# Layer one by products of halves, layer two with four hidden sums a tile pair, and a written-out step order, in a sigmoid attention and feed-forward kernel

## Chip, cores and metric

One core of a Trainium2 chip runs the whole program. The metric is the time on the device in microseconds, the median of several executions; beside it stands one execution that the hardware profiler recorded.

## What is computed

Sigmoid attention over 8 batches, 12 heads, 448 positions and 64 dimensions a head; its output, laid out as 3584 tokens of 768 values, goes through two dense layers with a gate between them. Inputs and output are float32 in HBM.

```python
scores = scale * q @ k.T - log(S)              # S = 448
attn   = sigmoid(scores) @ v                   # per batch and head
x      = attn.transpose(0, 2, 1, 3).reshape(3584, 768)
h      = x @ w_in                              # 768 -> 2048
g      = h * sigmoid(beta * h)
out    = g @ w_out                             # 2048 -> 768
```

## The kernel before

All matmuls run in fp16 with float32 sums. Heads are taken four at a time, a quad `g`; three quads make a batch `b`, 24 quads in all. For a quad, `transpose` (VectorE) turns the loaded q and k; `visit(g, jt)` makes the scores of key block `jt`: matmuls on 32 rows of the array, four side by side, into two score tiles (two PSUM buffers of two banks each), and `weigh` lets ScalarE apply the sigmoid into an `attnT` tile. `attend(g)` multiplies these with v, column tiles of 64, and VectorE casts the result into `xT`, which has six chunks of 128 channels by 448 tokens for a batch.

Layer one is `dense1(b, dc)`: for one of 16 blocks of 128 hidden columns, six matmuls of 448 columns (one a channel chunk) into a PSUM bank, a sigmoid on ScalarE and a multiplication on VectorE into `gt`. `gt` holds 896 tokens, seven tiles of 128, so batches alternate between its halves. For batch 0 the tokens are taken in two halves of 224.

Layer two takes token tiles in pairs. Tiles 0 and 1 are multiplied directly (`dense2`). Every later pair goes by Strassen's seven products of halves (`strassen`): the hidden dimension (16 blocks) and the 768 output columns are halved, each product is eight matmuls of 384 columns; weight sums T1, T3, T4, T6, T7 are formed once by `weight_sum`, five hidden sums a pair by `hidden_sum` on VectorE. Products are put together in `osb` on VectorE (one copy on ScalarE), then stored by DMAs that SP issues.

PSUM has four banks beside the score tiles; `bank` gives out the least recently used one that is not held, and `release` gives a held one back.

The order is fixed by the program. After the first batch's attention, a planner goes through the visits in order and puts filler work between them: a stream of `dense1`, `dense2` and `strassen` units with costs `M1_US`, `M1H_US`, `M2_US`, spread by a budget. Between the last visit of a quad and its `attend`, `dense` is cut into 64-column tiles (`tiled["cols"]`), as attention is. Each engine works through its own queue in program order. q, k, v and the weights are loaded by DMAs that POOL issues; before the change POOL does nothing else but a few memsets.

Of the kernel before, what the change touches and what calls it, by code (L numbers as in the profile page):

```python
# [8 lines left out]
FP32 = mybir.dt.float32  # L9
# [4 lines left out]
def kernel(  # L14
# [41 lines left out]
    qTp = ctx.enter_context(tc.tile_pool(name="qTp", bufs=4))  # L56
    kTp = ctx.enter_context(tc.tile_pool(name="kTp", bufs=4))
    attnp = ctx.enter_context(tc.tile_pool(name="attnp", bufs=12))
    xTp = ctx.enter_context(tc.tile_pool(name="xTp", bufs=3))
    sump = ctx.enter_context(tc.tile_pool(name="sump", bufs=3))  # L60
    sigp = ctx.enter_context(tc.tile_pool(name="sigp", bufs=3))
# [31 lines left out]
    beta_in = const.tile([BLK, P], FP32, name="beta_in")  # L93
# [128 lines left out]
    def weigh(sco, n: int):  # L222
        at = attnp.tile([P, 2, S], FP16, tag="attnT", name="attnT")
        nc.scalar.activation(  # L224
            out=at[:, :, 0:n],
            in_=sco[:, :, 0:n],
            func=AF.Sigmoid,
            bias=NEG_LOG_S,
            scale=MSCALE,
        )  # L230
        return at
# [18 lines left out]
    def half_visit(g: int, c0: int, second: int):  # L250
# [13 lines left out]
        ats = {id(sco): weigh(sco, n) for sco, n in zip(scos, widths)}  # L264
# [53 lines left out]

    def dense2(t: int, half: int, part: int):
        lo, hi = half * HALF, (half + 1) * HALF  # L320
        if part == 0:
            m2s[t, half] = bank("m2_ps", hi - lo, (t, half))
        m2 = m2s[t, half]
        for dc in range(part * NDC // N2, (part + 1) * NDC // N2):
            dense(
                m2,
                gt[:, dc, cols(t)],
                w_out16[:, dc, lo:hi],
                start=(dc == 0),
                stop=(dc == NDC - 1),  # L330
            )
        if part < N2 - 1:
            return
        release((t, half))
        if half == 0:
            osbs[t] = outp.tile([P, DM], FP32, tag="osb", name="osb")
        osb = osbs[t]
        nc.vector.tensor_copy(out=osb[:, lo:hi], in_=m2)
        if half == 1:
            store(t, 0, DM)  # L340
# [3 lines left out]
    def cols(t: int):  # L344
# [3 lines left out]

    ND = NDC // 2
    B11, B12, B21, B22 = (  # L350
# [4 lines left out]
    ws = {  # L355
        name: const.tile([P, ND, HALF], FP16, name=f"w_{name}")
        for name in ("T1", "T3", "T4", "T6", "T7")
    }

    def weight_sum(name: str, part: int):  # L360
        x, y, op = {
            "T1": (B11, B22, ALU.add),
            "T3": (B12, B22, ALU.subtract),
            "T4": (B21, B11, ALU.subtract),
            "T6": (B11, B12, ALU.add),
            "T7": (B21, B22, ALU.add),
        }[name]
        rows = slice(part * ND // 2, (part + 1) * ND // 2)
        nc.vector.tensor_tensor(out=ws[name][:, rows], in0=x[:, rows], in1=y[:, rows], op=op)
# [4 lines left out]

    def product(t: int, i: int):
        A11, A12, A21, A22 = hid(t, 0), hid(t, 1), hid(t + 1, 0), hid(t + 1, 1)
        return (
            ("r", A11, None, None, ws["T3"]),
            ("a", A22, None, None, ws["T4"]),
            ("s", A11, A12, ALU.add, B22),  # L380
            ("b", A21, A22, ALU.add, B11),
            ("a", A11, A22, ALU.add, ws["T1"]),
            ("r", A21, A11, ALU.subtract, ws["T6"]),
            ("a", A12, A22, ALU.subtract, ws["T7"]),
        )[i]

    NPROD = 7
    DIRECT = 2
    sums = {}

    def hidden_sum(t: int, i: int):
        _, x, y, op, _ = product(t, i)
        if op is not None:
            sums[t, i] = sump.tile([P, ND, P], FP16, tag="sum", name="sum")
            nc.vector.tensor_tensor(out=sums[t, i], in0=x, in1=y, op=op)  # L395

    def strassen(t: int, i: int, part: int):
        name, x, _, op, w = product(t, i)
        final = t == NT - 2
        if final and i == NPROD - 1:  # L400
            part = slice(part * HALF // 2, (part + 1) * HALF // 2)
            m2 = bank("m2_ps", HALF // 2)
            for dc in range(ND):
                dense(m2, sums[t, i][:, dc], w[:, dc, part], start=(dc == 0), stop=(dc == ND - 1))
            o1 = osbs[t]
            nc.vector.tensor_tensor(out=o1[:, part], in0=m2, in1=o1[:, part], op=ALU.add)  # L406
            store(t, part.start, part.stop)
            return
        if part == 0 and i + 2 < NPROD:
            hidden_sum(t, i + 2)  # L410
        first = (t, name) not in m2s
        if first:
            m2s[t, name] = bank("m2_ps", HALF, (t, name))
        m2 = m2s[t, name]
        for dc in range(part * ND // 2, (part + 1) * ND // 2):
            dense(
                m2,
                (x if op is None else sums[t, i])[:, dc],
                w[:, dc],
                start=first and dc == 0,  # L420
                stop=(dc == ND - 1),
                skip_group_check=i >= 4,
            )
            first = False if dc else first
        if part == 0:
            return
        if i == 0:
            for u in (t, t + 1):
                osbs[u] = outp.tile([P, DM], FP32, tag="osb", name="osb")
        L, R = slice(0, HALF), slice(HALF, DM)  # L430
        o1, o2 = osbs[t], osbs[t + 1]
        r, a = m2s.get((t, "r")), m2s.get((t, "a"))

        def add(out, in0, in1, op=ALU.add):
            nc.vector.tensor_tensor(out=out, in0=in0, in1=in1, op=op)  # L435

        if i == 1:
            nc.scalar.copy(out=o2[:, L], in_=a)  # L438
        elif i == 2:
            nc.vector.tensor_copy(out=o1[:, L], in_=m2)  # L440
            add(o1[:, R], r, o1[:, L])
            release((t, "s"))
            if final:
                store(t, HALF, DM)
        elif i == 3:
            add(o2[:, L], m2, o2[:, L])
            release((t, "b"))
            if final:
                store(t + 1, 0, HALF)
        elif i == 4:  # L450
            add(o2[:, R], a, o2[:, L], ALU.subtract)
            if final:
                add(o1[:, L], a, o1[:, L], ALU.subtract)
                release((t, "a"))
        elif i == 5:
            add(o2[:, R], r, o2[:, R])
            release((t, "r"))
            store(t + 1, HALF if final else 0, DM)
        elif i == 6:
            add(o1[:, L], a, o1[:, L], ALU.subtract)  # L460
            release((t, "a"))
            store(t, 0, DM)
# [16 lines left out]
    M1_US, M1H_US, M2_US, LEAST_US = 1.13, 0.58, 2.6, 2.0  # L479


    def second_layer(tiles):
        for t in tiles:
            if t < DIRECT:
                for half in range(2):
                    for part in range(N2):
                        yield M2_US / N2, lambda a=(t, half, part): dense2(*a), False
            elif t % 2 == 0:
                for i in range(NPROD):
                    for part in range(2):  # L490
                        yield M2_US / 4, lambda a=(t, i, part): strassen(*a), i in (2, 3) or (i, part) == (4, 0)

    def filler_stream():
        for c0 in (0, QH):
            for dc in range(NDC):
                yield M1H_US, 0, lambda dc=dc, c0=c0: dense1(0, dc, c0, QH), False
        for half in range(2):
            for t in range(DIRECT):
                for part in range(N2):
                    yield M2_US / N2, 0, lambda a=(t, half, part): dense2(*a), False  # L500
        for b in range(1, B):
            for dc in range(NDC):
                yield M1_US, QPB * (b + 1), lambda b=b, dc=dc: dense1(b, dc), False
            ends = [x * S // P // 2 * 2 for x in (b, b + 1)]
            for cost, unit, opens in second_layer(range(*ends)):
                yield cost, 0, unit, opens

    fill = list(filler_stream())
    at_fill = [0]

    def fill_units(n: int):
        for _ in range(n):
            fill[at_fill[0]][2]()
            at_fill[0] += 1

    def make_room():
        done = 0.0
        while len(held) > 1 and (len(held) > 2 or fill[at_fill[0]][3]):
            done += fill[at_fill[0]][0]
            fill_units(1)  # L520
        return done
# [4 lines left out]
    with tc.manual_schedule():  # L526
# [18 lines left out]
        still = const.tile([P, 512], FP16, name="still")  # L545
        nc.vector.memset(still, 0.0)
        nc.vector.memset(beta_in, 0.0)
# [57 lines left out]
        fill_units(4)  # L605
        half_visit(1, QH, 0)
        fill_units(3)
# [3 lines left out]
        fill_units(1)  # L611
        half_visit(2, QH, 0)
        fill_units(4)
        half_visit(2, QH, 1)
        attend(1, QH, QH)
        fill_units(3)
        attend(2, QH, QH)
        fill_units(1)
        transpose(QPB, 0)
        transpose(QPB, 1)  # L620
        fill_units(4)

        visits = [(QPB, jt, ()) for jt in range(JF + 1)]
        for g in range(QPB + 1, NQUAD, 2):
            visits += [(g, jt, ()) for jt in range(JF)] + [(g, JF, (g + 1,))]
            visits += [(g + 1, jt, ()) for jt in range(JF)]
# [77 lines left out]
```

## Time and profile before

| | |
|---|---|
| median of 3 runs | 382.3 us (382.11 to 383.91) |
| profiled execution | 381.98 us, of which its instructions span 380.2 us |
| TensorE clock granted | 1.0 throughout |
| busy: PE, VectorE, ScalarE, POOL | 375.0, 235.9, 229.2, 66.5 us |
| matmul instructions | 3435 recorded |
| longest wait of POOL | 176.4 us in total, loads of q waiting for a buffer that VectorE's transposes free |

In the profile PE is the matrix engine and PEld its weight loads, DVE is VectorE, ACT ScalarE, POOL GpSimd and SP the engine that issues the stores. L166 is line 166 of the kernel, the matmul inside `dense`, so all dense layers share that line and are told apart by their tiles; L213 is the scores, L279 attention, L224 the score sigmoid, L305 and L308 layer one's sigmoid and multiplication, L395 the hidden sums, L369 the weight sums, L435 the additions that put a pair together. Times of single instructions are durations; where an engine is pipelined, the distance between two starts is shorter.

### The profile page before, as it was taken

Reading aid. Unit: us, or ns where it says so; the run is one execution under the profiler, and the core shown is the slowest. Engines: PE = TensorE matmul, PEld = TensorE weight load, DVE = VectorE, ACT = ScalarE, POOL = GpSimd, SP = SyncE. Lnnn points to the kernel's source line nnn. Section 1 sums busy time; section 2 is a strip of 40 time slices with the busy share of each in tenths; the row PEclk is TensorE's granted clock in tenths of the full one; section 3 lists DMA queues with packets and bytes.
Section 4 is the critical chain, followed back from the end, with each engine's and each line's share of the span. In section 5 each row is a group of like instructions: output and inputs, shape, how many; then the busy total and the mean of one; then the engine's idle time right before and its main releaser. Section 6 shows DMA issues by size and latency. Waiting matters only on the chain.

```text
span 380.2 us, 8287 instructions
## 1 busy us (share of the span) xinstructions
PE 375.0 (99%) x3435; PEld 199.5 (52%) x3435; DVE 235.9 (62%) x448; ACT 229.2 (60%) x331; POOL 66.5 (17%) x114
## 2 busy tenths in 40 slices
PE   8999999999999999999999999999999999999996
PEld 3488744445454455544555445544545445555564
DVE  4357654977755667655676556655775665655675
ACT  5987975876447765377643786477554786405400
POOL 7735324041000410040110410122100000000000
PEclk9999999999999999999999999999999999999999
DMA  8999999591452932485341861439230300312023
GB/s 168 192 197 199 203 205 207 124 122 17 102 101 50 121 50 67 69 152 51 48 89 49 152 74 27 91 60 105 48 85 10 77 1 2 72 44 53 0 67 100
DMA packets 42693, 34.71 MB, mean 91 GB/s; under 512 B 21904, under 2 KB 39200, under 8 KB 42656
## 3 DMA queue, kind: packets, MB, share of 16 engines
q0 software_dynamic: 36688, 22.47, 43.1%
q1 hardware_dynamic: 5968, 11.71, 11.7%
q8 instruction: 27, 0.44, 0.5%
q14 instruction: 10, 0.08, 0.1%
HBM read 45.62 MB, written 11.01 MB: 149 GB/s over the span
## 4 chain that ended last, share of the span: by engine, by line
PE 97%; DMA 1%; ACT 1%; DVE 0%; SPq 0%; issue 0%
PE m_ps L166 74%; PE sco L213 12%; PE av_ps L279 10%; PE idle_ps L552 1%; DMA gt<-in_k_dram 1%; ACT attnT L224 1%; DVE kT L199 0%; ACT raw L558 0%; SPq L536 0%; DVE osb L406 0%
## 5 line engine op out<-in xcount | busy, mean ns | idle before, releaser
L224 ACT ACTIVATE attnT<-sco 128x896 f16<-128x896 f32 (+1 forms) x171 | 145.4, 903 | 80.7 <-PE sco L213 80.2
L166 PE MATMUL m_ps<-xT,w_in 128*128 128x448 f16 (+3 forms) x1008 | 154.4, 335 | 0.0
L308 DVE TENSOR_TENSOR gt<-m_ps,sg 128x448 f16<-128x448 f32 (+1 forms) x144 | 81.2, 572 | 74.4 <-ACT sg L305 71.4
L166 PEld LDWEIGHTS <-w_in 128*128 128x128 f16 (+1 forms) x1008 | 82.8, 101 | 68.2 <-issue 14.6
L305 ACT ACTIVATE sg<-m_ps,beta_sb 128x448 f32<-128x448 f32 (+1 forms) x144 | 84.2, 600 | 41.5 <-PE m_ps L166 34.7
L166 PEld LDWEIGHTS <-sum 128*64 128x64 f16 (+1 forms) x716 | 52.6, 104 | 35.7 <-issue 7.9
L166 PE MATMUL m_ps<-w_T,sum 128*128 128x384 f16 (+2 forms) x392 | 55.7, 323 | 0.0
L213 PE MATMUL sco<-qT,kT 32*128 32x448 f16 (+3 forms) x864 | 52.8, 340 | 0.8 <-DVE kT L199 0.5
L435 DVE TENSOR_TENSOR osb<-m_ps,osb 128x384 f32<-128x384 f32 x65 | 36.0, 555 | 20.4 <-PE m_ps L166 19.1
L110 POOL DMA_DIRECT2D raw<-in_q_dram x26 | 14.4, 553 | 181.8 <-DVE kT L203 176.4
L395 DVE TENSOR_TENSOR sum<-gt 128x1024 f16<-128x1024 f16 x65 | 42.6, 679 | 0.1
L279 PE MATMUL av_ps<-attnT,v 128*64 128x448 f16 (+3 forms) x432 | 40.2, 338 | 0.0
L288 DVE CAST xT<-av_ps 128x448 f16<-128x448 f32 (+1 forms) x54 | 28.5, 568 | 16.3 <-PE av_ps L279 15.2
L166 PEld LDWEIGHTS <-gt 128*64 128x64 f16 (+1 forms) x388 | 27.0, 105 | 20.5 <-issue 6.5
L166 PE MATMUL m_ps<-w_T,gt 128*64 128x384 f16 (+1 forms) x304 | 37.2, 327 | 0.0
L166 PE MATMUL m_ps<-w_out,sum 128*64 128x384 f16 (+1 forms) x324 | 36.5, 326 | 0.0
L279 PEld LDWEIGHTS <-v 128*64 128x64 f16 (+1 forms) x432 | 20.7, 108 | 18.6 <-issue 9.5
L213 PEld LDWEIGHTS <-kT 32*128 32x128 f16 (+1 forms) x864 | 13.9, 96 | 29.3 <-issue 27.0
L131 POOL DMA_DIRECT2D v<-in_v_dram x32 | 19.8, 630 | 14.0 <-DMA w_out<-in_moe_w_out_dram 6.7
L440 DVE COPY osb<-m_ps 128x384 f32<-128x384 f32 x13 | 7.3, 558 | 15.8 <-PE m_ps L166 15.8
L191 DVE STREAM_TRANSPOSE qT<-raw 128x448 f32<-128x448 f32 (+1 forms) x27 | 16.6, 615 | 0.1
L438 ACT COPY osb<-m_ps 128x384 f32<-128x384 f32 x13 | 6.3, 482 | 16.6 <-PE m_ps L166 16.6
(26 smaller groups left out, 94.0 us busy)
## 6 DMA issues: line engine op xcount, KB each, us to landing
out_dram<-osb SPq DMA_DIRECT2D x100, 96.0 KB, 1.9
raw<-in_k_dram POOLq DMA_DIRECT2D x23, 224.0 KB, 4.6
raw<-in_q_dram POOLq DMA_DIRECT2D x21, 224.0 KB, 3.8
v<-in_v_dram POOLq DMA_DIRECT2D x32, 144.0 KB, 6.3
w_in<-in_moe_w_in_dram POOLq DMA_DIRECT2D x8, 384.0 KB, 10.7
w_out<-in_moe_w_out_dram POOLq DMA_DIRECT2D x4, 768.0 KB, 13.0
v<-in_v_dram POOLq DMA_DIRECT2D x16, 48.0 KB, 5.9
out_dram<-osb SPq DMA_DIRECT2D x4, 192.0 KB, 1.9
```

Of the source, the lines that this page charges most:

```text
L110: nc.gpsimd.dma_start(out=raws[g][:, r, c0:c1].rearrange("p c d -> p (c d)"), in_=(q, k)[r][b, HQ * t : HQ * (t + 1)].rearrange("h (p c) d ...
L131: nc.gpsimd.dma_start(out=vs[b][i * BLK : (i + 1) * BLK, :, 0:JF].rearrange("p h j d -> p h (j d)"), in_=rows[:, :, JF * i * D : JF * (i + ...
L166: nc.tensor.matmul(to[c : c + step], hidden[:, c : c + step], weights, **({} if step == P else {"tile_position": (0, c)}), **flags,)
L191: nc.vector.transpose(out=in_order(g // QPB, qT[g][:, c0 * BLK : c1 * BLK]), in_=raw[:, c0:c1].rearrange("p c d -> p (c d)").bitcast(FP32),)
L213: nc.tensor.matmul(sco[base : base + nk, hh, u0 : u0 + n], kT[g][lo : lo + BLK, jt * P : jt * P + nk, e], qT[g][lo : lo + BLK, c0 : c0 + n ...
L224: nc.scalar.activation(out=at[:, :, 0:n], in_=sco[:, :, 0:n], func=AF.Sigmoid, bias=NEG_LOG_S, scale=MSCALE,)
L279: nc.tensor.matmul(av[hh * D : (hh + 1) * D, 0:n], vs[b][base : base + nk, 2 * (s % NPAIR) + hh, jt], at[base : base + nk, hh, 0:n], start ...
L288: nc.vector.tensor_copy(out=xTs[b][:, s % NPAIR, c0 : c0 + n], in_=av[:, 0:n])
L305: nc.scalar.activation(out=sg[:, 0:n], in_=m1[:, 0:n], func=AF.Sigmoid, bias=0.0, scale=beta_sb[:, dc : dc + 1])
L308: nc.vector.tensor_tensor(out=gt[:, dc, off : off + n], in0=m1[:, 0:n], in1=sg[:, 0:n], op=ALU.mult)
L395: nc.vector.tensor_tensor(out=sums[t, i], in0=x, in1=y, op=op)
L435: nc.vector.tensor_tensor(out=out, in0=in0, in1=in1, op=op)
```

## The change

Layer one of batches 2 to 7 (`wino1`, step I) goes by Winograd's form of Strassen's seven products: channels (six chunks), tokens (448) and hidden columns (2048) are each halved. For a group `d` of four column blocks (two in either half), each product is 2 x 3 matmuls of 224 columns. Four weight sums S1 to S4 are formed once (S3 over `w_in`), four token sums a batch (`token_sum`, step X) by VectorE. The products are combined through four PSUM banks x, y, w, z and two `osb` buffers: ScalarE copies P1, VectorE adds P6, P5, P7, P3, P4; the left half of the upper block is multiplied on VectorE, the other three quarters (`weigh_right`, step G, and `weigh_below`, step B) get their sigmoid from SBUF and are multiplied on POOL.

Layer two (`wino2`, step U) keeps seven products a pair, in the same form: four hidden sums (step H) for five, three weight sums T2 to T4 and T1 written over `w_out`.

The planner is gone. All steps behind the first batch's attention stand in a table of 746 steps, done in that order by `follow`: V visit, A attend, D `dense1`, O `dense2`, I `wino1` (batch, group, product), U `wino2` (tile, product, half), R transpose, E copy of v's last block, Q and K loads, X, H, G, B, S and T sums. Buffers are cut elsewhere (q and k three for four, `attnT` nine for twelve), and the early half visits put part of their weights into `osb` buffers.

```diff
-    qTp = ctx.enter_context(tc.tile_pool(name="qTp", bufs=4))
-    kTp = ctx.enter_context(tc.tile_pool(name="kTp", bufs=4))
-    attnp = ctx.enter_context(tc.tile_pool(name="attnp", bufs=12))
+    qTp = ctx.enter_context(tc.tile_pool(name="qTp", bufs=3))
+    kTp = ctx.enter_context(tc.tile_pool(name="kTp", bufs=3))
+    attnp = ctx.enter_context(tc.tile_pool(name="attnp", bufs=9))
     xTp = ctx.enter_context(tc.tile_pool(name="xTp", bufs=3))
     sump = ctx.enter_context(tc.tile_pool(name="sump", bufs=3))
-    sigp = ctx.enter_context(tc.tile_pool(name="sigp", bufs=3))
+    sigp = ctx.enter_context(tc.tile_pool(name="sigp", bufs=4))
+    xsp = ctx.enter_context(tc.tile_pool(name="xsp", bufs=1))
...
-    def weigh(sco, n: int):
-        at = attnp.tile([P, 2, S], FP16, tag="attnT", name="attnT")
+    def weigh(sco, n: int, at=None):
+        if at is None:
+            at = attnp.tile([P, 2, S], FP16, tag="attnT", name="attnT")
...
+        homes = [None, None]
+        if c0 == 0 and g < QPB - 1:
+            home = outp.tile([P, 2 * S], FP32, tag="osb", name="early")
+            home = home.bitcast(FP16).rearrange("p (x h s) -> p x h s", x=2, h=2)
+            homes = [home[:, x] for x in range(2)]
+        ats = {id(sco): weigh(sco, n, at) for sco, n, at in zip(scos, widths, homes)}
...
+    BANK = {"P1": "x", "P2": "x", "P6": "y", "P5": "w", "P3": "w", "P7": "z", "P4": "z"}
+    OPENS = ("P1", "P6", "P5", "P7")
...
+    T2, T3, T4 = (const.tile([P, ND, HALF], FP16, name=f"w_T{i}") for i in (2, 3, 4))
+    T1 = B12
+    A11, A12, A21, A22 = (
+        w_in16[:, c * NK : (c + 1) * NK, r * DH : (r + 1) * DH] for r in range(2) for c in range(2)
+    )
+    S1, S2, S4 = (const.tile([P, NK, DH], FP16, name=f"w_S{i}") for i in (1, 2, 4))
+    S3 = A21
...
+            "T3": (T3, B22, B12, ALU.subtract),
+            "T2": (T2, T3, B11, ALU.add),
+            "T4": (T4, B21, T2, ALU.subtract),
+            "T1": (T1, B12, B11, ALU.subtract),
+            "S1": (S1, A21, A22, ALU.add),
+            "S2": (S2, S1, A11, ALU.subtract),
+            "S4": (S4, A12, S2, ALU.subtract),
+            "S3": (S3, A11, A21, ALU.subtract),
...
+    def token_sum(b: int, i: int):
+        x = xTs[b]
+        b11, b12 = x[:, 0:NK, 0:QH], x[:, 0:NK, QH:S]
+        b21, b22 = x[:, NK:NHC, 0:QH], x[:, NK:NHC, QH:S]
+        if i == 0:
+            xs[b] = xsp.tile([P, 3, NK, QH], FP16, tag="xs", name="xs")
+        t = xs[b]
+        out, in0, in1 = (
+            (t[:, 0], b12, b11),
+            (t[:, 1], b22, t[:, 0]),
+            (b12, b22, b12),
+            (t[:, 2], b21, t[:, 1]),
+        )[i]
+        add(out, in0, in1, ALU.subtract)
...
+    def wino1(b: int, d: int, p: str):
+        x, t = xTs[b], xs.get(b)
+        lhs, rhs = {
+            "P1": lambda: (A11, x[:, 0:NK, 0:QH]),
+            "P2": lambda: (A12, x[:, NK:NHC, 0:QH]),
+            "P3": lambda: (S4, x[:, NK:NHC, QH:S]),
+            "P4": lambda: (A22, t[:, 2]),
+            "P5": lambda: (S1, t[:, 0]),
+            "P6": lambda: (S2, t[:, 1]),
+            "P7": lambda: (S3, x[:, 0:NK, QH:S]),
+        }[p]()
+        key = (b, d, BANK[p])
+        opens = p in OPENS
+        if opens:
+            m2s[key] = bank("m1_ps", S, key)
+        m = m2s[key].rearrange("p (q n) -> p q n", q=2)
+        for j in range(2):
+            for hc in range(NK):
+                nc.tensor.matmul(
+                    m[:, j],
+                    lhs[:, hc, (2 * d + j) * P : (2 * d + j + 1) * P],
+                    rhs[:, hc],
+                    start=opens and j == 0 and hc == 0,
+                    stop=hc == NK - 1,
+                    skip_group_check=True,
+                )
+        off = (b % 2) * S
+        if p == "P1":
+            for n in "ab":
+                o = outp.tile([P, 2 * S], FP32, tag="osb", name="osb")
+                osbs[b, d, n] = o.rearrange("p (h q n) -> p h q n", h=2, q=2)
+        oa, ob = osbs[b, d, "a"], osbs[b, d, "b"]
+
+        if p == "P1":
+            nc.scalar.copy(out=oa[:, 0], in_=m)
+        elif p == "P6":
+            add(oa[:, 0], m, oa[:, 0])
+        elif p == "P5":
+            add(oa[:, 1], m, oa[:, 0])
+        elif p == "P7":
+            add(oa[:, 1], m, oa[:, 1])
+        elif p == "P2":
+            for j in range(2):
+                sigmoid(ob[:, 1, j], m[:, j], 2 * d + j)
+        elif p == "P3":
+            add(ob[:, 0], m, oa[:, 0])
+            first = m2s[b, d, "x"].rearrange("p (q n) -> p q n", q=2)
+            nc.vector.tensor_tensor(
+                out=gt[:, 2 * d : 2 * d + 2, off : off + QH], in0=first, in1=ob[:, 1], op=ALU.mult
+            )
+            release((b, d, "x"))
+        elif p == "P4":
+            add(oa[:, 0], m, oa[:, 0])
+        if p not in ("P1", "P5", "P7", "P2"):
+            release(key)
...
+    def weigh_right(b: int, d: int):
+        ob = osbs[b, d, "b"]
+        sg = sigp.tile([P, S], FP32, tag="sg", name="sg").rearrange("p (q n) -> p q n", q=2)
+        for j in range(2):
+            sigmoid(sg[:, j], ob[:, 0, j], 2 * d + j)
+        off = (b % 2) * S + QH
+        nc.gpsimd.tensor_tensor(
+            out=gt[:, 2 * d : 2 * d + 2, off : off + QH], in0=ob[:, 0], in1=sg, op=ALU.mult
+        )
+
+    def weigh_below(b: int, d: int, j: int):
+        oa = osbs[b, d, "a"]
+        dc = ND + 2 * d + j
+        sg = sigp.tile([P, S], FP32, tag="sg", name="sg").rearrange("p (h n) -> p h n", h=2)
+        sigmoid(sg, oa[:, :, j], dc)
+        off = (b % 2) * S
+        nc.gpsimd.tensor_tensor(
+            out=gt[:, dc, off : off + S].rearrange("p (h n) -> p h n", h=2),
+            in0=oa[:, :, j],
+            in1=sg,
+            op=ALU.mult,
+        )
...
+        if i == 0:
+            add(sums[t, 0], a21, a22)
+        elif i == 1:
+            add(sums[t, 1], sums[t, 0], a11, ALU.subtract)
+        elif i == 2:
+            add(sums[t, 2], a11, a21, ALU.subtract)
+        else:
+            add(sums[t, 1], a12, sums[t, 1], ALU.subtract)
...
+    def wino2(t: int, p: str, part: int):
+        lhs, rhs = {
+            "P1": lambda: (hid(t, 0), B11),
+            "P2": lambda: (hid(t, 1), B21),
+            "P3": lambda: (sums[t, 1], B22),
+            "P4": lambda: (hid(t + 1, 1), T4),
+            "P5": lambda: (sums[t, 0], T1),
+            "P6": lambda: (sums[t, 1], T2),
+            "P7": lambda: (sums[t, 2], T3),
+        }[p]()
+        key = (t, BANK[p])
...
+        if p == "P1":
+            nc.vector.tensor_copy(out=o2[:, L], in_=m2)
+        elif p == "P6":
             add(o2[:, L], m2, o2[:, L])
-            release((t, "b"))
-            if final:
-                store(t + 1, 0, HALF)
-        elif i == 4:
-            add(o2[:, R], a, o2[:, L], ALU.subtract)
-            if final:
-                add(o1[:, L], a, o1[:, L], ALU.subtract)
-                release((t, "a"))
-        elif i == 5:
-            add(o2[:, R], r, o2[:, R])
-            release((t, "r"))
-            store(t + 1, HALF if final else 0, DM)
-        elif i == 6:
-            add(o1[:, L], a, o1[:, L], ALU.subtract)
-            release((t, "a"))
-            store(t, 0, DM)
+        elif p == "P5":
+            add(o2[:, R], m2, o2[:, L])
+        elif p == "P7":
+            add(o2[:, R], m2, o2[:, R])
+            if last:
+                store(t + 1, HALF, DM)
+        elif p == "P2":
+            nc.scalar.copy(out=o1[:, L], in_=m2)
+            if last:
+                store(t, 0, HALF)
+        elif p == "P3":
+            add(o1[:, R], m2, o2[:, L])
+            store(t, HALF if last else 0, DM)
+        elif p == "P4":
+            add(o2[:, L], m2, o2[:, L])
+            store(t + 1, 0, DM)
+        if p in ("P6", "P2", "P3", "P4"):
+            release(key)
...
+    ALSO = {g: (g + 1,) if g > QPB and g + 1 < NQUAD else () for g in range(QPB, NQUAD)}
+    RUN = {
+        "V": lambda g, jt: visit(g, jt, ALSO[g] if jt == JF else ()),
+        "A": lambda g: attend(g, 0, S),
+        "D": lambda b, dc: dense1(b, dc, 0, S) if b else dense1(0, dc, QH, QH),
+        "O": dense2,
+        "I": lambda b, d, i: wino1(b, d, f"P{i}"),
+        "U": lambda t, i, part: wino2(t, f"P{i}", part),
+        "R": transpose,
+        "E": double_v_last,
+        "Q": load_qk,
+        "K": load_v,
+        "X": token_sum,
+        "G": weigh_right,
+        "B": weigh_below,
+        "H": hidden_sum,
+        "S": lambda i, part: weight_sum(f"S{i}", part),
+        "T": lambda i, part: weight_sum(f"T{i}", part),
+    }
...
+    def follow(steps):
+        nearer = [""] * len(steps)
+        for i in reversed(range(len(steps) - 1)):
+            nxt = steps[i + 1][0]
+            nearer[i] = nxt if nxt in "VA" else nearer[i + 1]
+        for step, then in zip(steps, nearer):
+            tiled["cols"] = D if then == "A" else P
+            RUN[step[0]](*(int(x) for x in step[1:].split(".")))
...
+    STEPS = """
+        R3.0 R3.1 D0.9 D0.0 D0.6 S1.0 Q6 S2.0 V3.0 D0.14 D0.8 V3.3 D0.7 D0.2 R4.1 D0.11 D0.15 V3.1
...
+        R9.1 V8.1 R9.0 U2.5.1 H2.3 H4.0 U2.7.0 U2.7.1 V8.3 U2.3.0 X2.0 U2.3.1 S3.0 A8 V9.1 X2.2 X2.1
+        R10.1 U2.4.0 U2.4.1 I2.0.1 I2.0.6 X2.3 I2.0.5 V9.0 I2.0.7 H4.1 I2.0.2 I2.0.3 H4.2 Q11 G2.0
+        I2.0.4 V9.2 U4.6.0 B2.0.0 R10.0 Q12 U4.1.0 U4.1.1 U4.5.0 U4.6.1 V10.1 E3 U4.2.0 H4.3 A9
+        B2.0.1 V10.0 U4.5.1 U4.2.1 U4.7.0 U4.7.1 S2.1 U4.3.0 I2.1.1 U4.3.1 V10.2 R11.1 U4.4.0 U4.4.1
+        I2.1.6 I2.1.5 I2.1.2 R11.0 K4 I2.1.7 I2.1.3 V10.3 I2.1.4 Q13 G2.1 I2.2.1 S3.1 B2.1.0 B2.1.1
+        S4.1 A10 V11.1 I2.2.6 I2.2.5 I2.2.7 I2.2.2 I2.2.3 I2.3.1 I2.2.4 Q16 G2.2 B2.2.0 I2.3.6
+        I2.3.5 B2.2.1 I2.3.7 I2.3.2 I2.3.3 V11.0 I2.3.4 H6.2 U6.1.0 R12.0 U6.1.1 B2.3.0 B2.3.1 R12.1
+        Q14 H6.0 V11.2 U6.7.0 U6.2.0 U6.2.1 H6.1 X3.0 A11 G2.3 V12.0 U6.6.0 U6.6.1 X3.1 I3.0.1
...
+        I7.1.5 I7.1.7 I7.1.2 I7.1.3 G7.1 I7.2.1 I7.1.4 B7.1.0 I7.2.6 B7.1.1 I7.2.5 I7.2.7 I7.2.2
+        I7.3.1 I7.2.3 I7.2.4 G7.2 B7.2.1 I7.3.6 I7.3.5 I7.3.7 I7.3.2 I7.3.3 I7.3.4 B7.2.0 U24.1.0
+        B7.3.0 H24.2 U24.1.1 U26.1.0 B7.3.1 U24.7.0 U24.2.0 H24.0 U24.2.1 G7.3 H24.1 U24.5.0 U24.6.0
+        U24.6.1 H24.3 U24.5.1 U24.7.1 U26.1.1 H26.2 H26.0 U24.3.0 U24.4.0 U24.3.1 U26.2.0 H26.1
+        U26.5.0 U26.2.1 U26.6.0 U26.7.0 U26.6.1 H26.3 U26.5.1 U26.7.1 U24.4.1 U26.3.0 U26.3.1
+        U26.4.0 U26.4.1
+    """.split()
...
-        visits = [(QPB, jt, ()) for jt in range(JF + 1)]
-        for g in range(QPB + 1, NQUAD, 2):
-            visits += [(g, jt, ()) for jt in range(JF)] + [(g, JF, (g + 1,))]
-            visits += [(g + 1, jt, ()) for jt in range(JF)]
...
+        follow(STEPS)
```

## The prediction

> **What bounds the kernel now.** I read the page first: busy shares, granted clock and the chain that ended last.
>
> ```profile
> span 380.2 us, 8287 instructions
> PE 375.0 (99%) x3435; PEld 199.5 (52%) x3435; DVE 235.9 (62%) x448; ACT 229.2 (60%) x331; POOL 66.5 (17%) x114
> PEclk9999999999999999999999999999999999999999
> PE 97%; DMA 1%; ACT 1%; DVE 0%; SPq 0%; issue 0%
> ```
>
> The matrix engine works from start to end at full clock, and the chain is 97% its own work. A busy PE need not be PE at its best pace, so the next question is what sets its pace; the timeline answers, PE alone, two stretches (start us, length us, what, count).
>
> ```profile
> 33.22 3.05 PE L166 MATMUL m_ps<-xT,w_in 128*128 128x224 f16 x30
> 36.20 0.57 PE L213 MATMUL sco<-qT,kT 32*128 32x448 f16 x8
> ...
> 66.70 3.57 PE L166 MATMUL m_ps<-xT,w_in 128*128 128x448 f16 x18
> 70.20 0.58 PE L213 MATMUL sco<-qT,kT 32*128 32x448 f16 x8
> 70.71 3.58 PE L166 MATMUL m_ps<-xT,w_in 128*128 128x448 f16 x18
> ```
>
> One 448-column matmul lasts 353 ns and one of 224 columns 259 ns (mean ns by form, below), but they overlap. Steps: (3.57 - 0.35)/17 = 0.189 us for 448 columns and (3.05 - 0.26)/29 = 0.096 us for 224. So 224 columns with a weight load each cost almost exactly half. A change of tile shape costs extra: 18 x 0.189 = 3.40, but the scores start 70.20 - 66.70 = 3.50 later, so 0.10; and 36.20 - 33.22 - 30 x 0.096 = 0.10. PE's time is therefore a sum of steps and shape changes, with next to no waits: in the list of waits the longest of PE itself is 1.2 us, at the start.
>
> Then the groups by form (busy us, mean ns, idle before) and busy time by stretch, for what the other engines have left.
>
> ```profile
> L305 ACT ACTIVATE sg<-m_ps,beta_sb 128x448 f32<-128x448 f32 x112 | 71.3, 637 | 38.0 <-PE m_ps L166 34.5
> L308 DVE TENSOR_TENSOR gt<-m_ps,sg 128x448 f16<-128x448 f32 x112 | 69.7, 624 | 64.5 <-ACT sg L305 61.5
> L395 DVE TENSOR_TENSOR sum<-gt 128x1024 f16<-128x1024 f16 x65 | 42.6, 679 | 0.1
> L166 PEld LDWEIGHTS <-w_in 128*64 128x64 f16 x288 | 15.4, 110 | 12.9 <-issue 3.8
> L166 PE MATMUL m_ps<-xT,w_in 128*128 128x224 f16 x186 | 19.5, 259 | 0.0
> L369 DVE TENSOR_TENSOR w_T<-w_out 128x1536 f16<-128x1536 f16 x10 | 9.1, 941 | 0.0
> L305 ACT ACTIVATE sg<-m_ps,beta_sb 128x224 f32<-128x224 f32 x32 | 12.9, 470 | 3.5 <-DVE xT L288 1.1 <-DVE beta_sb L593 1.1 <-PE m_ps L166 0.2
> L438 ACT COPY osb<-m_ps 128x384 f32<-128x384 f32 x13 | 6.3, 482 | 16.6 <-PE m_ps L166 16.6
> ```
> ```profile
> 70.00:80.00 10.00, 10.00 (x90) 4.63 (x90) 9.38 (x16) 8.97 (x13) 3.47 (x6) 1.00 0.40 74
> ```
>
> Note the last line: from 70 to 80 us VectorE is busy 9.38 and ScalarE 8.97 of 10 us while PE stays full. Their queues hold slack; a loaded engine is no PE wait by itself.
>
> **The change on PE.** A group d of a batch covers four blocks of 128 hidden columns. Before: 4 x 6 = 24 matmuls of 448 columns, 24 x 0.189 = 4.54 us. After (wino1): 7 products x 2 x 3 = 42 matmuls of 224 columns, 42 x 0.096 = 4.03 us. Six batches of four groups: 24 x 0.504 = **12.1 us less**. Layer two keeps 7 products of 8 matmuls of 384 columns a pair (13 pairs before and after), the direct tiles 0 and 1, batches 0 and 1 of layer one, scores and attention keep their matmuls: 0. Shape changes: wino1 is never cut into 64 columns as `dense` is ahead of an attention; but the table puts only U, O and D steps just before an A step. Along PE's order I count 170 changes in the trace from 33.3 us on and 174 in the table's order: 4 x 0.10 = **0.4 us more**. With no new wait: 381.98 - 12.1 + 0.4 = 370.3 us.
>
> **The change on the others (hidden unless PE waits).**
> - VectorE, a group: P6, P5, P7, P3, P4 add and one multiplication, 6 x 0.624 = 3.74 us for 4 x 0.624 = 2.50: 24 x 1.25 = 30 us more. Token sums: 24 of 672 fp16 elements, on the line through 679 (1024) and 941 ns (1536) 0.50 each: 12 more. Hidden sums, four for five a pair: 13 x 0.68 = 8.8 less. Weight sums, 16 parts for 10: 5.6 more. Pair evictions: five adds and a copy as before, 0. In all 235.9 + 39 = 275 of 368 us, 75%.
> - ScalarE, a group: one copy (482 at 384 columns, about 0.53 at 448), four sigmoids of 224 (4 x 0.47) and two of 448 (2 x 0.637): 3.69 for 2.55, 24 x 1.14 = 27 more: 257, 70%. Sigmoids that now read SBUF show in no row; from 0.47 to 0.637 for 224 would add 48 x 0.17 = 8, still 72%.
> - POOL gets 72 multiplications of 448 columns. No row shows arithmetic there. The ends: 0.48, the shortest row of such a size on any engine (ScalarE's copy), and 1.25, twice VectorE's 0.624 for this same product, should the two operands be taken one after the other. I take 0.94, halfway between 0.624 and its double, as nothing tells these apart: 68 us more, 134 us, 36%. By the Trainium skill, GPSIMD Engine Reference, section 3.1, a two-input operation of 2048 fp32 elements takes 4497 ns, so an estimate of 1.0 us, with which the tail below would come out 0.2 us later; no run here shows it yet.
> - Queues. Products stand on POOL behind the loads of Q (2 issues of 0.55) and K (6 of 0.62, 3.7 us). A Q step comes after the transposes that free its buffer, so nothing is held there; K4 and Q13 ahead of G2.1 delay its product and the two of B2.1 by up to 4.8 us, but their first reader, H6.0, is some 12 us of PE work further. Before, only loads stood there. SP's stores keep their number and size. Where ScalarE's copy of P1 waits for an `osb` buffer (four, now shared by layer one and two), the score sigmoids are queued behind it, and the next scores wait for those.
>
> **What the new waits cost.** PE now depends on VectorE inside a group: four PSUM banks carry x, y, w, z, and P2, P3, P4 write into banks that ScalarE or VectorE must have read. A group gives VectorE 3.74 us of work in 4.03 us of PE time, so undiluted groups leave 0.3 us. The table mixes them with U, V and A steps. I cut the table into stretches of 5 us of PE work (0.096, 0.163 for 384 columns, 0.189 and 0.10 a change) and summed VectorE's durations in each: 13 of 66 exceed their PE time, by 5.3 us in all (worst: around X2.0 to U4.6.0, 1.2 us over ten). That is the upper end of this cost, 0 the lower. Rows of single durations overstate a busy queue, and the stretch at 70 to 80 us shows PE full beside 9.38; I take a quarter, **1.3 us**. No gain can hide here, as PE has no waits to lose.
> The tail is the one place without scores to fill. After I7.3.4 the result takes 0.26, its add 0.62, the sigmoids B7.3.0 and B7.3.1 2 x 0.64, to 2.16; POOL is still in the product before, started about 0.64; three products in line end at 0.64 + 0.94, 2.5 and 3.4. U24.2.1 reads the last; ahead of it stand U24.1.0, 1.1, U26.1.0, U24.7.0, U24.2.0, 5 x 0.65 = 3.26. A wait of 0.2, at 1.25 one of 1.1, at 0.62 none; with H24.0 behind it I take **0.7**. The final stores are as before.
> Sum: 381.98 - 12.1 + 0.4 + 1.3 + 0.7 = **372.3 us**. The profiled run stands 0.3 under the median of 382.3, so I say 372.5; differences of about 0.5% (1.9 us) are what a measurement of this kernel can tell from none.
>
> **Rivals.**
> 1. The queues absorb everything: 370.3 to 370.6. For it: PE full at 70 to 80 us. Against: the tail. 0.12.
> 2. The dense stretches cost their full 5.3 and, with ScalarE late behind buffer waits (its stretches are over by 8.0 us in all), half of that again, 4.0: 370.3 + 5.3 + 4.0 + 1.1 = 380.7 at worst; as a case 376 to 380. 0.18.
> 3. **VectorE becomes the bound, slower.** A batch gives VectorE: groups 15.0, token sums 2.0, hidden sums 6.5 x 0.68 = 4.4, pair evictions 5.4, attention casts 3.7, transposes 4.4, doubling 0.4: 35.3 us for 43.3 us of PE work. There are 10.5 sums a batch that read two SBUF operands, and 12 products on POOL. If each sum stood still for a product, VectorE gains 10.5 times its length: at 0.77 us it equals PE, from 0.95 on the whole gain is gone, at 1.25 it ends at 48.4 and the kernel at 370.3 + 6 x 5.1 = 401. Against: products fill 11.3 of 43.3 us, so one sum in four meets one, half over: 0.12 us each. 388 as its middle. 0.08. The Trainium skill, SBUF — State Buffer, section "Who interferes with whom", has such a rule: a VectorE instruction with two SBUF inputs and a GpSimd one that reads SBUF lock each other out; no run here shows it, and by that rule alone the meeting sums would add 1.3 us a batch.
> 4. The weight loads set the pace of 224 columns: at 110 ns, the row of loads of 64 columns, a group takes 42 x 0.110 = 4.62, and the kernel 381.98 + 24 x 0.084 + 0.4 = 384.4. Against: thirty loads and matmuls in a row at 0.096 above. 0.02. The Trainium skill, TensorE: Matmul & The Clock Gate, section "LDWEIGHTS (loading the stationary operand)", gives columns / 1.2, an estimate of 107 ns and 381.4 us; the trace's 0.096 decides against it.
> 5. The saving is there but matched by waits: 380.4 to 384. 0.03.
>
> **How the numbers follow.** Forecast 0.57 (370.6 to 376), rival 1 0.12, rival 2 0.18, rivals 3 and 4 0.10, rival 5 0.03. Faster 0.57 + 0.12 + 0.18 = 0.87; same 0.03; slower 0.10. The range reaches from 369.8, rival 1 less half a microsecond of scatter, to 379.5, most of rival 2, which leaves out rivals 3 to 5 and a little: 0.15 or so.
>
> **What would show it.** Right: 1008 matmuls of 224 columns more and 576 of 448 fewer, at steps of 0.096 us; PE near 97% busy, its waits a few us in all, on VectorE (P3, P4, next P6) and at U24.2.1 or U24.5.0; VectorE near 275 us. Wrong: PE waits over 6 us, hidden or token sums much longer than 0.68 and 0.50 beside POOL's products (rival 3), steps of 224 over 0.1 us (rival 4), or scores waiting for ScalarE.

## The result

The changed kernel takes 379.4 us (median of 9 runs) where the kernel before takes 382.7 beside it: ratio 0.992, interval [0.990, 0.995]. One of the nine runs of the kernel before took 428 us, far above the others, and the ratio is formed without it. The changed kernel is faster, but by 3.3 us where 10 were forecast. The profiled run took 379.15 us.

From its page, the lines that answer to those of before:

```profile
span 377.4 us, 8887 instructions
PE 365.4 (97%) x3567; PEld 234.8 (62%) x3567; DVE 275.2 (73%) x512; ACT 249.2 (66%) x403; POOL 149.4 (40%) x186
PEclk9999999999999999999999999999999999999999
PE 70%; DVE 12%; DMA 6%; POOL 4%; issue 4%; ACT 3%; SPq 0%; DVEq 0%; POOLq 0%; ACTq 0%
```

The clock is as before. The chain has changed its nature: 97% PE before, 70% now, with VectorE, transfers, POOL and ScalarE in between. The list of waits of PE alone (us in total, times, longest us) read before:

```profile
PE idle_ps L552 <- DVE still L546: 1.2, 1, 1.2
PE sco L213 <- DVE kT L199: 0.5, 1, 0.5
PE sco L213 <- ACT attnT L224: 0.2, 1, 0.2
```

The first of these is at the start, and none is longer than 0.5 us after it. Now the list reads in part:

```profile
PE m_ps L166 <- DVE osb L362: 1.4, 2, 0.8
...
PE m_ps L437 <- DVE gt L466: 1.2, 4, 0.7
...
PE m_ps L166 <- DVE osb L563: 0.8, 1, 0.8
PE m_ps L166 <- DVE gt L466: 0.7, 3, 0.3
PE m_ps L166 <- DVE sum L362: 0.4, 1, 0.4
PE m_ps L166 <- POOL gt L491: 0.3, 1, 0.3
```

These idle times understate it, as the end of a matmul is modelled. A better count is the distance between neighbouring starts beyond the step (0.096, 0.163, 0.189 us) and 0.10 for a change of shape; summing those over 0.12, from the first scores on, I call it PE's waits. Before: 0.8 us. After: 10.3 us. Without them PE's work from the first scores to the last matmul is 376.74 - 5.75 - 0.8 = 370.2 before and 373.94 - 5.78 - 10.3 = 357.9 after: 12.3 us less, as the sum had it. The loss is all waits, in three kinds:

- 4.4 us in 12 waits where a product or pair opens a PSUM bank right behind a group's P4 or the P1 after it.
- 3.3 us in six waits of layer two, where VectorE or POOL comes late, with a sum or with the reading of a bank.
- 0.7 us in the split last product, and 1.9 us in small ones, 1.3 of them before 45 us.

One wait of the first kind, in the timeline of the changed kernel (start us, length us, what; in brackets idle time and what ended it):

```profile
221.30 0.74 PE L437 MATMUL m_ps<-xs,w_in 128*128 128x224 f16 x6
...
221.53 0.61 DVE L466 TENSOR_TENSOR gt<-m_ps,osb 128x448 f16<-128x448 f32 x1
...
222.20 0.74 PE L437 MATMUL m_ps<-xs,w_S 128*128 128x224 f16 x6 [0.17 <-DVE gt L466]
```

The first line is P4; its last matmul starts at 221.78, so the next could start at 221.87. It waits to 222.20 for the multiplication L466, which reads bank x, P1 and P2 of the group just left, until 222.14: the new product has been given that bank.

And by form, what the others' work came to (busy us, mean ns | idle before):

```profile
L362 DVE TENSOR_TENSOR osb<-m_ps,osb 128x448 f32<-128x448 f32 x120 | 74.2, 620 | 19.1 <-PE m_ps L437 10.6 <-ACT osb L453 2.1 <-ACT attnT L225 2.0
L491 POOL TENSOR_TENSOR gt<-osb,sg 128x448 f16<-128x448 f32 x48 | 54.5, 1147 | 67.3 <-ACT sg L415 62.4 <-issue 4.6
L437 PE MATMUL m_ps<-xT,w_in 128*128 128x224 f16 x432 | 49.8, 259 | 0.1
L362 DVE TENSOR_TENSOR sum<-gt,sum 128x1024 f16<-128x1024 f16 x13 | 10.1, 777 | 0.1
L362 DVE TENSOR_TENSOR xs<-xT 128x672 f16<-128x672 f16 x6 | 6.1, 1016 | 0.0
L141 DVE COPY v<-v 64x768 f16<-64x768 f16 x8 | 4.6, 576 | 4.0 <-DMA v<-in_v_dram 3.8
L362 DVE TENSOR_TENSOR xT<-xT 128x672 f16<-128x672 f16 x6 | 3.0, 498 | 0.0
```

Two sums of the same 672 elements take 498 and 1016 ns on the mean, and the copy of v, 360 ns before, 576. The timeline shows why:

```profile
143.75 1.13 POOL L481 TENSOR_TENSOR gt<-osb,sg 128x448 f16<-128x448 f32 x1 [0.26 <-ACT sg L415]
143.81 1.45 DVE L362 TENSOR_TENSOR xs<-xT 128x672 f16<-128x672 f16 x1
```

The sum begins 0.06 us behind a GpSimd product and ends 0.37 behind its end: it stood until the product was nearly done. This is the meeting that the prediction's third rival needed. It is the rule in this trace: 11 of the 76 hidden and token sums and 2 of the 8 copies of v are stretched, each begins while a product runs, and each ends a fixed time behind that product, 0.36 to 0.37 us for 672 elements, 0.55 for 1024, 0.21 to 0.22 for the copy. The additions that read one operand from PSUM show nothing of it: the 52 that overlap a product by more than 0.02 us take 0.621 us on the mean, the 68 others 0.620.

Such a stretched sum can reach PE, as here:

```profile
244.41 1.13 POOL L491 TENSOR_TENSOR gt<-osb,sg 128x448 f16<-128x448 f32 x1 [6.58 <-ACT sg L415]
244.45 1.64 DVE L362 TENSOR_TENSOR sum<-gt,sum 128x1024 f16<-128x1024 f16 x1
...
246.01 0.55 DVE L362 TENSOR_TENSOR osb<-m_ps,osb 128x384 f32<-128x384 f32 x1
...
246.61 1.17 PE L166 MATMUL m_ps<-w_out,sum 128*64 128x384 f16 x12 [0.84 <-DVE osb L362]
```

The hidden sum takes 1.64 us for 0.68, the addition queued behind it comes late, and PE waits for that addition.

### The profile page after: what moved, and what is told of

Read it like the earlier page. It is cut to its first block, busy times and chain, and to the rows that moved or that the text cites. A ratio compares the mean times of both kernels' runs of the same rounds, so it can differ in the third digit from the quotient of the medians.

```text
span 377.4 us, 8887 instructions
## 1 busy us (share of the span) xinstructions
PE 365.4 (97%) x3567; PEld 234.8 (62%) x3567; DVE 275.2 (73%) x512; ACT 249.2 (66%) x403; POOL 149.4 (40%) x186
## 4 chain that ended last, share of the span: by engine, by line
PE 70%; DVE 12%; DMA 6%; POOL 4%; issue 4%; ACT 3%; SPq 0%; DVEq 0%; POOLq 0%; ACTq 0%
PE m_ps L166 36%; PE m_ps L437 18%; PE sco L213 8%; PE av_ps L285 8%; DVE osb L362 6%; DMA w_in<-in_moe_w_in_dram 3%; POOL gt L491 2%; DVE gt L466 2%; DMA raw<-in_k_dram 2%; DVE sum L362 2%; ACT attnT L225 1%; POOL w_in L148 1%; DVE xs L362 1%; ACT sg L415 1%; POOL raw L110 1%
## 5 line engine op out<-in xcount | busy, mean ns | idle before, releaser
L362 DVE TENSOR_TENSOR osb<-m_ps,osb 128x448 f32<-128x448 f32 (+1 forms) x186 | 109.8, 594 | 48.1 <-PE m_ps L166 27.8
L491 POOL TENSOR_TENSOR gt<-osb,sg 128x448 f16<-128x448 f32 x48 | 54.5, 1147 | 67.3 <-ACT sg L415 62.4
L481 POOL TENSOR_TENSOR gt<-osb,sg 128x448 f16<-128x448 f32 x24 | 28.7, 1198 | 79.3 <-ACT sg L415 69.2
L437 PEld LDWEIGHTS <-w_in 128*128 128x128 f16 x576 | 54.2, 98 | 8.7 <-issue 5.7
L415 ACT ACTIVATE sg<-osb,beta_sb 128x224 f32<-128x224 f32 (+1 forms) x96 | 50.4, 571 | 8.7 <-DVE osb L362 8.7
L166 PE MATMUL m_ps<-w_out,gt 128*128 128x384 f16 (+1 forms) x346 | 52.5, 327 | 1.3 <-DVE osb L563 0.8
L437 PE MATMUL m_ps<-xT,w_in 128*128 128x224 f16 x432 | 49.8, 259 | 0.1
L437 PEld LDWEIGHTS <-w_S 128*128 128x128 f16 x432 | 40.9, 97 | 6.8 <-issue 5.5
L166 PE MATMUL m_ps<-w_out,sum 128*128 128x384 f16 (+1 forms) x244 | 40.6, 327 | 1.2 <-DVE osb L362 0.8
L166 PE MATMUL m_ps<-w_T,sum 128*128 128x384 f16 (+1 forms) x228 | 40.5, 327 | 0.9 <-DVE gt L466 0.7
L166 PEld LDWEIGHTS <-w_in 128*128 128x128 f16 (+1 forms) x294 | 26.6, 98 | 12.6 <-issue 3.4
```

The lines of the kernel that those rows point to most:

```text
L166: nc.tensor.matmul(to[c : c + step], hidden[:, c : c + step], weights, **({} if step == P else {"tile_position": (0, c)}), **flags,)
L415: nc.scalar.activation(out=out, in_=in_, func=AF.Sigmoid, bias=0.0, scale=beta_sb[:, dc : dc + 1])
L437: nc.tensor.matmul(m[:, j], lhs[:, hc, (2 * d + j) * P : (2 * d + j + 1) * P], rhs[:, hc], start=opens and j == 0 and hc == 0, stop=hc == ...
L481: nc.gpsimd.tensor_tensor(out=gt[:, 2 * d : 2 * d + 2, off : off + QH], in0=ob[:, 0], in1=sg, op=ALU.mult)
L491: nc.gpsimd.tensor_tensor(out=gt[:, dc, off : off + S].rearrange("p (h n) -> p h n", h=2), in0=oa[:, :, j], in1=sg, op=ALU.mult,)
```

## Experiments

The theory after the traces: two causes, each on its own, **bank turn** (a bank is given out again while VectorE reads it) and **port** (GpSimd's products hold up VectorE's sums with two operands in SBUF, and the products' own results come late). The rival: VectorE simply has too much work in these stretches (**load**), and any relief helps alike. All ratios are to the kernel before on the same chip.

**1. Bank turn alone.** In P3 of `wino1` the banks change the order in which they are given back:

```diff
         elif p == "P3":
             ...
-            release((b, d, "x"))
         ...
         if p not in ("P1", "P5", "P7", "P2"):
             release(key)
+        if p == "P3":
+            release((b, d, "x"))
```

> Bank theory: in the changed kernel the next group's P6 gets the PSUM bank x that the left-half multiplication (L466) still reads, because x is given back before w; waits behind P4 sum to about 4.2 us. Giving w back first hands P6 the bank that was read one instruction (0.62 us) earlier, so most of these waits go: 2 to 4 us less than the changed kernel's 379.4, about 376.5. Load theory (VectorE has too much work in these stretches whatever the bank): under 1 us less, 378.5 to 379.4. Port theory (GpSimd products hold up sums): no difference.

Measured: 376.1 us, ratio 0.983 [0.982, 0.985], 3.3 us under the changed kernel. PE's waits fall from 10.3 to 5.6 us. The same place in its timeline:

```profile
220.76 0.74 PE L437 MATMUL m_ps<-xs,w_in 128*128 128x224 f16 x6
...
221.00 0.61 DVE L466 TENSOR_TENSOR gt<-m_ps,osb 128x448 f16<-128x448 f32 x1
...
221.34 0.74 PE L437 MATMUL m_ps<-xs,w_S 128*128 128x224 f16 x6
```

P6 follows P4 after 0.58, six steps of 0.096, while L466 still runs: it has another bank. Of the waits behind P4 one is left, of 0.37 us, and a few new ones of 0.16 to 0.45 us stand around P3. VectorE's work is the same (274.4 us busy for 275.2), so load alone is not the cause.

**2. The last product whole.** `if last and p == "P4"` is made never true, so the product is not split into halves.

> The last product of the last pair is done whole, 384 columns, not in two halves of 192. Theory: the halves share one bank, and the second half's matmuls wait 0.68 us for the first half's addition; whole, PE takes 1.30 us without a wait, then one addition of 0.55 for 0.36: 0.4 to 0.6 us less than the changed kernel, near 378.9. Rival: the split pays as it did before, and the whole product is 0.3 us slower.

Measured: 380.2 us, ratio 0.994 [0.993, 0.996]. No gain is seen, so the theory fell. From the start of this product to the end of the span the changed kernel takes 377.4 - 372.0 = 5.4 us with the wait, the whole one 379.2 - 373.6 = 5.6: the shorter last addition and store pay for the wait.

**3. No GpSimd products.** `weigh_right` and `weigh_below` let ScalarE write the sigmoid into `gt`; the kernel leaves out the multiplications on GpSimd.

> Leaves out the gate's product h * sigmoid for the three quarters that GpSimd multiplies (the sigmoid goes straight into gt); its time tells what the 72 products on GpSimd cost beyond PE. Port theory: the sums with two SBUF operands lose their stretching (6.2 us of VectorE time, and 1.7 us of the copies of v), and the late hidden sums (3.3 us of PE waits) go: 3 to 4 us less than the changed kernel, about 376. Bank theory: the 4.2 us behind P4 stay, so not under 375. If the products are hidden anyway: within 0.5 us of 379.4.

Measured: 375.8 us, ratio 0.984 [0.982, 0.985], 3.6 under the changed kernel. The sums and the copy of v have lost their stretching, and the wait shown above at 246.6 us is gone; the waits behind P4 are still there (3.9 us of a total of 6.3):

```profile
L362 DVE TENSOR_TENSOR sum<-gt,sum 128x1024 f16<-128x1024 f16 x13 | 8.8, 680 | 0.1
L362 DVE TENSOR_TENSOR xs<-xT 128x672 f16<-128x672 f16 x6 | 3.0, 498 | 0.0
L141 DVE COPY v<-v 64x768 f16<-64x768 f16 x8 | 2.8, 354 | 4.0 <-DMA v<-in_v_dram 3.8
```

**4. No left multiplication.** ScalarE writes P2's sigmoid into `gt`; the kernel leaves out L466.

> Leaves out the gate's product for the left upper quarter (ScalarE writes the sigmoid straight into gt): 24 multiplications of 0.61 us less on VectorE, and bank x is free after ScalarE's second sigmoid. Bank theory: as much as giving w back first or a little more, 3 to 5 us less, about 375.5. Load theory: 14.7 us less work on VectorE, 3 to 5 us less too, but then giving w back first brings nothing. Port theory: under 1 us.

Measured: 374.8 us, ratio 0.981 [0.979, 0.983], 4.6 less. No wait behind P4 is left. The medians put it 1.3 us below experiment 1, but the two intervals overlap and its profiled span is no shorter (373.4 us for 373.0), so it isn't shown that 14.7 us fewer multiplications on VectorE add anything to the freed bank. If load counts here, it is the smaller part.

**5. Layer one by `dense1` in the table.** A `dense1` block stands at the place of products 1, 5, 2 and 3 of each group; the sums and products that only layer one's halves need are left out:

```diff
+        at = {"1": (0, 0), "5": (0, 1), "2": (1, 0), "3": (1, 1)}
...
+                if i in at:
+                    low, j = at[i]
+                    yield f"D{b}.{low * ND + 2 * int(d) + j}"
+            elif step[0] not in "GBXS":
+                yield step
```

> The table and layer two as changed, layer one of batches 2 to 7 by dense1 as before (at the places of products 1, 5, 2 and 3; no token sums, no S sums, no GpSimd products). If the 12.1 us per-matmul saving of layer one is right and the table and layer two cost PE nothing by themselves: 381 to 383, like the kernel before, with PE waits near its 0.4 us. If the table or layer two brings waits of its own: 384 or more, and the loss would not be layer one's.

Measured: 387.4 us, ratio 1.013 [1.012, 1.015]. A miss by 5 us: PE's waits are 4.9 us, half of them inside and between visits (0.67, 0.67, 0.34, 0.30, 0.30, 0.23), for a transposed q or a score tile that ScalarE still reads, and PE's work is 0.8 over that of before. So this order without its products is worse than the planner's, and the run can't price the table by itself. It does give what the products are worth in this order: 8.0 us, 13 off PE's work and 5 lost to more waits.

**6. Both causes away.** Experiments 1 and 3 together.

> Giving w back first and no GpSimd products (the gate's product is left out for three quarters of the units). If bank turn and port are two separate causes of the waits, the gains of the two alone, 3.3 and 3.6 us, add: 372.0 to 373.0, near the 370.3 to 372.5 that the sum without and with small waits gave. If both only relieve the same VectorE load: 374.5 to 375.8.

Measured: 371.9 us, ratio 0.972 [0.970, 0.974]. The gains add (3.3 + 3.6 = 6.9, measured 7.6, a little under the expected 372.0), so they are two causes and not one load: VectorE is still busy 267.9 us, 72% of the span, and PE's waits are 2.1 us. The list of PE's waits is down to three rows of the first 40 us and the wait inside the last product:

```profile
PE sco L213 <- DVE kT L199: 1.4, 2, 1.1
PE idle_ps L712 <- DVE gt L705: 1.2, 1, 1.2
PE m_ps L166 <- DVE osb L362: 0.5, 1, 0.5
PE sco L213 <- ACT attnT L225: 0.2, 1, 0.2
```

**7. Products into a scratch tile.** GpSimd multiplies as before, but into `sg`, which nobody reads; ScalarE writes the sigmoid into `gt`, so the product is left out of the result.

> GpSimd does the same 72 products but into a scratch tile, and the sigmoid goes straight into gt (so the gate's product is left out there): the port is as busy as before, but nobody waits for a product except for its buffers. If the loss is the sums held up by the products (port): near the changed kernel, 378 to 379.5, with the sums still stretched over 1 us here and there. If the loss is hidden sums that wait for late products (lateness): near 376, as without products.

Measured: 378.0 us, ratio 0.989 [0.987, 0.991], 1.4 under the changed kernel and 2.2 over experiment 3. The intervals of the two do not overlap, so the 2.2 us are clear: more than half of the products' cost comes without anyone waiting for their results, which leaves the port. These products read the sigmoid in fp16 and are a little shorter (1.06 and 1.08 us on the mean for 1.15 and 1.20), so it is rather under- than overstated. The remaining 1.4 us fit hidden sums that wait for late products, as the tail's waits of 0.43 and 0.56 us are gone from this trace, but here the intervals overlap. The sums are still stretched:

```profile
L362 DVE TENSOR_TENSOR sum<-gt,sum 128x1024 f16<-128x1024 f16 x13 | 9.9, 761 | 0.1
L362 DVE TENSOR_TENSOR xs<-xT 128x672 f16<-128x672 f16 x6 | 4.8, 797 | 0.0
```

**8 and 9. A mended version.** Experiment 1, the last group's two lower products on VectorE, a bank of its own for the first half of the very last product, and small moves in the table. Of the edit, the second part:

```diff
-        nc.gpsimd.tensor_tensor(
+        engine = nc.vector if (b, d) == (B - 1, 3) else nc.gpsimd
+        engine.tensor_tensor(
```

> A version of the changed kernel with the waits mended that the traces name: w given back first; the last group's two lower products on VectorE, which idles there (waits of 0.45 and 0.56 us at U24.2.1 and U24.6.0); the first half of the very last product in a bank of its own (0.68 us); two token sums of batch 5 moved behind V18.2 and U14.2.1 (0.85 us at U14.2.0). If each wait is its own: 376.1 - 2.5 = 373.6. If VectorE's load only moves them: 375 to 376.

Measured: 374.6 us, ratio 0.980 [0.978, 0.983]. The tail's wait at U24.2.1 is gone, but the moved token sum made P7 of batch 5 wait 0.98 us for it, and the bank for the first half took the second half's wait only from 0.68 to 0.61.

> The mended version once more, with the two moves that failed replaced: the token sums of batch 5 stay, and instead the copy of v's last block of batch 6 (E6, 1.18 us beside a GpSimd product, 0.36 without) goes behind H14.2; the transpose R16.1 goes behind I3.2.4 (wait of 0.45 at I3.2.3); one lower product of batch 6 is on VectorE (wait of 0.41 at U20.5.0); of the last product the second half, not the first, gets the fresh bank. If the waits are separate: 376.1 - 0.85 - 0.45 - 0.4 - 1.0 - 0.5 = 372.9. If VectorE's queue moves them on: 374 to 375, no better than the 374.6 of the version before.

Measured: 374.7 us, ratio 0.980 [0.977, 0.983], PE's waits 4.7 us. No wait of the last product is left and U14.2.0 waits 0.47 for 0.85, but others came back: 0.43 at the P3 of the next group where 0.45 had been, and 0.60 for 0.40 at a P3 of batch 5. Each move gives less than its own wait, as the rival had it: here VectorE's queue does move the waits on. Both versions beat the kernel before by 2.0% and the changed one by 1.3 to 1.4%; over experiment 1, whose interval overlaps theirs, the 1.5 us are not shown.

**10. The bar.** The changed kernel again beside the last one.

> The changed kernel unaltered, beside the mended one on the same chip: 378.7 to 380 by every theory; it serves as the bar for the mended one.

Measured: 379.9 us, ratio 0.993 [0.991, 0.996].

## Why the prediction was right and wrong

The matrix engine's own saving was right; what failed is the term for the new waits. The measured 379.4 us lies at the far edge of the stated range, 369.8 to 379.5, and two of the prediction's own signs of being wrong came true: PE's waits are over 6 us, and sums are much longer beside products on POOL.

- **PE's saving**: 12.1 less 0.4 forecast, 12.3 measured in PE's work. 224 columns step by 0.096 us (1137 distances, median 0.096); changes of shape 175, forecast 174, for 170. Right; rival 4 is out. Its 110 ns was the row of loads of 64 columns; the rows of loads of 128 columns have 98 ns, before as after.
- **The others' work**: VectorE 275 forecast, 275.2 measured; that the two agree to 0.2 is luck, as the stretched sums are in the measured figure alone, and without products on GpSimd it is 267.8 (experiment 3). Additions of 448 columns take 0.620, 0.624 forecast. ScalarE 257 forecast, 249 measured. POOL 134 forecast, 149 measured, as a product takes 1.14 us in the median (1.15 and 1.20 on the mean of the two lines), near the upper end of 1.25, not the 0.94 taken. The lower end of 0.48 was not the shortest row: a VectorE cast of 448 columns takes 0.39 us in the kernel before. The estimate of 1.0 us worked out from the Trainium skill's figure (GPSIMD Engine Reference, section 3.1) is below the measured 1.14 too.
- **What the new waits cost**: this is the step that failed, 1.3 + 0.7 us forecast, 9.5 measured (10.3 after, 0.8 before). Sums over stretches of 5 us asked only if VectorE has time, not whether its result is there when PE comes. For bank x the rows would have told: behind P3 its result takes 0.26, its addition 0.62 and L466 0.61, 1.49 us; the next group's P6 comes after P4 and P1, 2 x 0.576 = 1.15 us later, and `bank` hands it x, given back first. A wait of 0.34 at each turn with nothing in between; measured 0.26 to 0.49 in most, 0.90 in one, 4.4 in all.
- **The tail**: a wait at U24.2.1 and one for H24.0 forecast, 0.7; measured 0.43 at U24.2.1 and 0.56 at U24.5.0, plus 0.16 at U24.7.0, with the products at their real length: 1.15 for 0.7. Its mechanism was right. That the last product's halves share a bank was not seen, but it costs nothing that the whole product would not.
- **The port**: rival 3's mechanism is real and stood at 0.12 us a sum, as an average. The measured excess is 6.3 us over 76 sums, 0.08 each, so the size was nearly right; wrong was to put it at nothing in the forecast's sum. It comes in 11 pieces of up to 0.95 us, and some of those land ahead of results that PE waits for: about 2.2 of the 3.6 us that the products cost, by experiments 3 and 7. Nor does it need two operands in SBUF: the copy of v, which reads one, takes 1.18 and 1.31 us beside products and 0.35 without. The Trainium skill, SBUF — State Buffer, section "Who interferes with whom", has a VectorE instruction with two SBUF inputs contend with a GpSimd one that reads SBUF, under an exclusive lock. The traces agree for the sums: 498 ns in experiment 3, without products, 797 in experiment 7 and 1016 in the changed kernel.
- **The time** fell into rival 2's case, 376 to 380, at 0.18, by waits on VectorE, but not by its mechanism: dense stretches as such were the smaller part, with 2.1 us of waits left in experiment 6 under nearly the same load. ScalarE's waits for stores came to 3.4 us in two places, but of PE's waits only 0.5 us are for ScalarE. That the time fell into this case is luck.

## What to carry to other kernels

When a chain of products shares a few accumulator banks, follow each bank by hand from its last reader to the next product that opens it; a load sum over microseconds can't show a wait of a third of one that comes back at every turn. The order in which banks are given back can be worth more than the engines' load: two moved lines brought here as much as the change itself. Work put on GpSimd because it idles is not free where VectorE forms sums of two SBUF operands or copies within SBUF; count the meetings in whole instruction lengths.

## What the runs showed of the hardware

A VectorE sum of two SBUF operands that begins 0.06 us behind a GpSimd product lasts 1.45 us for 0.50, and the copy of v 1.18 and 1.31 for 0.35 in two places; additions with one operand in PSUM stay at 0.62 us. The product can be held up too, when the sum begins first: 7 of 72 take 1.28 to 1.58 us for 1.14. A float32 product of 448 columns lasts 1.14 us in the median on GpSimd and 0.61 on VectorE, which takes one operand from PSUM.
